# Part of one weight matrix moves from the SyncE queue's even spread to two GpSimd DMAs on seven DMA engines

## The chip, the cores and the metric

The kernel runs on one core of a Trainium2 chip. The metric is device time in microseconds (us) of one execution; lower is better. Before the change the median of three runs is 405.4 us (405.32 to 405.54).

## The reference

One decoding step (batch 1, one new token, model width 1024) of two blocks that share an input and whose outputs are added:

```
xn  = layernorm(x)                                   # 1024
A   = attention(xn @ wq, k_cache, v_cache) @ wo      # 32 query heads, 4 key/value heads, 65536 keys, 128 wide
B   : h  = gelu(layernorm(xn) @ w1)                  # 1024 x 1024
      hs = concat(four quarters of h, each shifted along the sequence and padded with zeros) @ w2   # 1024 x 1024
      x1 = xn + hs
      B  = x1 + gelu(layernorm(x1) @ w3) @ w4        # 1024 x 3584, 3584 x 1024
out = x + A + B
```

The sequence has length 1, so every shift by one or two positions leaves only the zero padding: the vector that is multiplied by w2 is zero, whatever h is. The kernel computes that product all the same. The data are bf16. Keys and values are 64 MiB each; the weights together are some 36 MB. All of it is read once.

## The kernel before

Everything is a stream of loads from HBM into eight buffers ("slots") of 128 partitions by 8192 bf16 values (16 KiB on each partition, 2 MiB in all), issued by SyncE in a fixed order: wq (two loads of two slots), w1, w2, w3 (two of two slots), then the four heads' keys and values in loads of two slots (4 MiB), where keys run five loads ahead of values, with wo's quarters among the last value loads, and w4 at the end. `issue` (it is called after each use of a slot) issues a load as soon as its slots are free, that is, when the TensorE or VectorE work that read the slot's last contents has signalled. So SyncE waits for slots, and up to eight slots of loads are queued on the DMA engines at any time. The last parts of w4 are issued in small pieces with a semaphore each (`load_pieces`, L306), so that its matmuls can begin piece by piece.

Uses go in the same order on the other engines. `rows_mv` (L424) multiplies a vector by rows of a weight matrix: partition p of a slot holds R = 8 consecutive rows, row kk of each is the moving operand, and four column ranges of 256 go to four row groups of PSUM. `to_p` (L428) brings the result back to partitions. Keys are transposed by VectorE into the tile `X` (two halves, L501) before TensorE takes them (L509); values are used from the slot (L549). `X` is [128, 2, 8192] bf16; half 1 also serves `to_p` (as `X32`, the same bytes seen as f32), and half 0 is first written when the first keys come.

`load_w2` does not exist yet: w2 is one load of one slot, `load(w2_v[:, 0:SLOT])` (L282), each partition taking 8 rows, 16 KiB in one run. `use_w2` multiplies it by `g_bf`, a tile of zeros that GpSimd clears at the start (the zero padding of the reference), and forms x1 and its layer norm.

GpSimd clears and fills constants at the start (L353 to L374) and computes one power in each of three layer norms (L410). ScalarE's queue issues the two loads of x: `xP_bf` (128 partitions of 16 bytes) and `xr_bf` (four partitions, 0, 32, 64 and 96, of 512 bytes), the second after VectorE has cleared `xr_bf` (L379). The first layer norm waits for both.

A wait before an instruction comes from `_deps`: it waits for the semaphores that stand in the buffers' records of writes and reads.

Of the kernel before, what the change touches and what calls it, by code (L numbers as in the profile page):

```python
# [6 lines left out]
BF = mybir.dt.bfloat16  # L7
F32 = mybir.dt.float32
# [66 lines left out]
def _deps(q, reads, writes):  # L75
    for b in reads:
        for s, v in b.w.items():
            q.wait((s, v))
    for b in writes:
        for s, v in b.w.items():  # L80
            q.wait((s, v))
        for s, v in b.r.items():
            q.wait((s, v))


def _done(ev, reads, writes, partial=False):
    for b in reads:
        b.add_read(ev)
    for b in writes:
        if partial:  # L90
            b.add_write(ev)
        else:
            b.set_write(ev)


def _op(q, fn, reads=(), writes=(), partial=False):
    _deps(q, reads, writes)
    ev = q.op(fn, True)
    _done(ev, reads, writes, partial)
    return ev  # L100


def _grp(q, fns, reads=(), writes=(), partial=False):
    _deps(q, reads, writes)
    ev = None
    for i, fn in enumerate(fns):
        ev = q.op(fn, i == len(fns) - 1)
    _done(ev, reads, writes, partial)
    return ev
# [8 lines left out]
def _dma(q, chan, fn, reads=(), writes=(), partial=False):  # L118
    _deps(q, reads, writes)
    chan.n += 1  # L120
    ev = q.dma(fn, chan.sem, 16 * chan.n)
    _done(ev, reads, writes, partial)
    return ev
# [10 lines left out]
def bass_parallel_sum__gqa_block_cached__mixer_s_mlp__decode_kernel(  # L134
# [14 lines left out]
    P = 128  # L149
    D = A_x.shape[2]  # L150
# [5 lines left out]
    R = D // P  # L156
# [6 lines left out]
    RW = D // 4  # L163
# [2 lines left out]
    SCALE = float(DH) ** -0.5  # L166
    EPS = 1e-5
    NS = 8
    SLOT = 8192

    with ExitStack() as es:
# [3 lines left out]
        def sb(name, shape, dt):  # L175
            return E(nc.sbuf_tensor(name, shape, dt))

        def ps(name, shape, dt):
            return E(nc.psum_tensor(name, shape, dt))

        def sem(name):
            return E(nc.semaphore(name))
# [24 lines left out]
        Yall = sb("Yall", [P, HKV, 4, 4, G], BF)  # L207
        slots_sb = sb("slots_sb", [P, NS, SLOT], BF)
        X = sb("X", [P, 2, SLOT], BF)
        S_sb = sb("S_sb", [P, NCH, 512], F32)  # L210
# [15 lines left out]
        g_bf = sb("g_bf", [P, R + 32], BF)  # L226
# [2 lines left out]
        ge_b = sb("ge_b", [P, NT], F32)  # L229
        h1g_bf = sb("h1g_bf", [P, R], BF)  # L230
        gh_bf = sb("gh_bf", [P, NT + 32], BF)
        fin = sb("fin", [P, RW], BF)

        S_all = ps("S_ps", [P, 4 * 512], F32)
# [4 lines left out]
        M1_ps = ps("M1_ps", [P, 512], F32)  # L239

        q_pe = _Q("pe", sem("c_pe"))
        q_dve = _Q("dve", sem("c_dve"))
        q_act = _Q("act", sem("c_act"))
        q_pool = _Q("pool", sem("c_pool"))
        q_sp = _Q("sp", None)
        ch_x = _DmaChan(sem("d_x"))
        ch_out = _DmaChan(sem("d_out"))
        slots = [_Slot(slots_sb[:, i, :], _B("slot%d" % i), _DmaChan(sem("d_s%d" % i))) for i in range(NS)]

        b_const = _B(); b_xb = _B(); b_x = _B(); b_xn = _B(); b_xn2 = _B(); b_x1 = _B(); b_xn3 = _B()  # L250
        b_ln = _B(); b_qT = _B(); b_Y = _B(); b_misc = _B(); b_ge = _B()
        b_X = [_B(), _B()]
# [5 lines left out]
        b_p = _B(); b_pT = _B(); b_lcol = [_B(), _B()]; b_OL = _B(); b_O = _B()  # L258
        b_cb = _B(); b_oP = [_B() for _ in range(HKV)]
        b_xr = _B(); b_accr = _B(); b_h1 = _B(); b_gh = _B(); b_fin = _B()  # L260


        place = [0]
        n_load = [0]
        taken = [0] * NS

        def room(n):
            p0 = place[0] + (place[0] % 2 if n == 2 else 0)
            return p0, all(taken[(p0 + i) % NS] == 0 for i in range(n))

        def take(n, uses):
            p0, free = room(n)
            assert free
            place[0] = p0 + n
            for i in range(n):
                taken[(p0 + i) % NS] = uses
            return p0 % NS

        def load(src, width=SLOT):
            i = take(1, 1)  # L280
            view = slots_sb[:, i, 0:width]
            _dma(q_sp, slots[i].chan, lambda e, view=view, src=src: e.dma_start(out=view, in_=src), writes=[slots[i].buf])  # L282
            return [(view, [slots[i].buf], i)]

        def load2(src, half=SLOT):
            i = take(2, 1)
            view = slots_sb[:, i:i + 2, :].rearrange("p s c -> p (s c)")[:, 0:2 * half]
            if 2 * half < 2 * SLOT:
                for k in range(2):
                    taken[i + k] = 2  # L290
            _dma(q_sp, slots[i].chan, lambda e, view=view, src=src: e.dma_start(out=view, in_=src), writes=[slots[i].buf, slots[i + 1].buf])  # L291
            bufs = [[slots[i].buf], [slots[i + 1].buf]] if half == SLOT else [[slots[i].buf, slots[i + 1].buf]] * 2
            return [(view[:, k * half:(k + 1) * half], bufs[k], i + k) for k in range(2)]
# [16 lines left out]

        wq_v = A_wq.rearrange("(p r) n -> p (r n)", p=P)
        w1_v = B_w1.rearrange("(p r) n -> p (r n)", p=P)
        w2_v = B_w2.rearrange("(p r) n -> p (r n)", p=P)
        w3_v = B_w3.rearrange("(p r) n -> p (r n)", p=P)
        w4_v = B_w4.rearrange("(p r) n -> p (r n)", p=P)

# [30 lines left out]
            return load2(A_v_cache[0, h, a * n:(a + 1) * n, :].rearrange("(p c) d -> p (c d)", p=P))  # L347


        evs = []  # L350
        for t_, val in ((selGT_bf, 1.0), (selTT, 1.0), (ident_bf, 0.0), (ones_f, 1.0), (neghalf, -0.5), (permWE, 1.0), (maskA, 1.0),
                        (sel16, 1.0), (dmask, 0.0), (g_bf, 0.0), (xn_bf, 0.0), (xn2_bf, 0.0), (xn3_bf, 0.0), (oP_bf, 0.0), (gh_bf, 0.0)):
# [22 lines left out]
                                                          compare_op=ALU.not_equal, fill=1.0, base=-16 * j, channel_multiplier=1))  # L375
        b_const.set_write(ev)

        _dma(q_act, ch_x, lambda e: e.dma_start(out=xP_bf[:, :], in_=A_x[0, 0, :].rearrange("(p r) -> p r", p=P)), writes=[b_xb])
        _op(q_dve, lambda e: e.memset(xr_bf[:], 0.0), writes=[b_xr])  # L379
        _dma(q_act, ch_x, lambda e: e.dma_start(out=xr_bf[0:P:32, :], in_=A_x[0, 0, :].rearrange("(j m) -> j m", j=4)), writes=[b_xr])  # L380
# [8 lines left out]
        def late_consts():  # L389
            _op(q_dve, lambda e: e.tensor_scalar(out=Lmat[:], in0=M1_ps[:, 0:P], scalar1=-SCALE, scalar2=None, op0=ALU.mult), reads=[b_M1], writes=[b_sel], partial=True)  # L390
            _op(q_dve, lambda e: e.tensor_copy(selT_f[:], M1_ps[:, 136:140]), reads=[b_M1], writes=[b_sel], partial=True)
            _op(q_dve, lambda e: e.tensor_copy(selL[:, :, :], M1_ps[:, P:P + 8].unsqueeze(2).broadcast_to([P, G, 16])), reads=[b_M1], writes=[b_sel], partial=True)
        xstep = X[:].ap[0][0]
        X32 = X[:].bitcast(F32)

        def layer_norm(src, b_src, dst_f, dst_bf, b_dst, c0):
            _op(q_dve, lambda e: e.reduce_sum(ln_s[:, 0:1], src[:], axis=AX.X), reads=[b_src], writes=[b_ln])
# [20 lines left out]
        def rows_mv(nkk, parts, st_fn, b_st, b_slot, b_out, first, last, k0=0):  # L418
            fns = []
            for kk in range(k0, k0 + nkk):  # L420
                for out_fn, mv_fn in parts:
                    for j in range(4):
                        fns.append(lambda e, kk=kk, j=j, out_fn=out_fn, mv_fn=mv_fn, st=(first and kk == k0), sp=(last and kk == k0 + nkk - 1):
                                   e.matmul(out_fn(j), st_fn(kk), mv_fn(kk, j), start=st, stop=sp, tile_position=(0, 32 * j), skip_group_check=True))  # L424
            _grp(q_pe, fns, reads=b_slot + [b_st], writes=b_out, partial=not first)

        def to_p(src, c0, n, b_src):
            _op(q_dve, lambda e: e.transpose(out=X32[:, 1, c0:c0 + 32 * n], in_=src), reads=b_src, writes=[b_X[1]], partial=c0 > 0)  # L428

# [9 lines left out]
        def use_wq(j, ld):  # L439
# [7 lines left out]
            for hf in range(2):  # L447
                to_p(S_ps[hf][:, :], 512 * hf, 16, [b_S[hf]])
            _op(q_dve, lambda e: e.tensor_copy(qT_bf[:], X32[:, 1, 0:1024:32]), reads=[b_X[1]], writes=[b_qT])
            _grp(q_pe, [lambda e, we=we: e.matmul(M0_ps[:, 128 + 32 * we:128 + 32 * we + HQ], permWE[:, we, :], qT_bf[:, :], start=True, stop=True)  # L450
# [8 lines left out]
        def d_parts(view, c0):  # L459
            return [(lambda t: M1_ps[32 * t:32 * t + 32, c0:c0 + RW], lambda kk, t: view[:, kk * D + t * RW:kk * D + (t + 1) * RW])]  # L460
# [6 lines left out]

        def use_w2(ld):
            view, b = ld[0:2]
            rows_mv(R, d_parts(view, 0), lambda kk: g_bf[:, kk:kk + 32], b_const, b, [b_M1], True, False)  # L470
            to_p(M1_ps[:, 0:RW].rearrange("p (c r) -> p r c", r=R), 0, R, [b_M1])
            _op(q_dve, lambda e: e.tensor_tensor(out=x1[:], in0=xn[:], in1=X32[:, 1, 0:32 * R:32], op=ALU.add), reads=[b_xn, b_X[1]], writes=[b_x1])
            layer_norm(x1, b_x1, None, xn3_bf, b_xn3, 4)
# [22 lines left out]
        def use_k(h, ch, ld):  # L496
# [3 lines left out]
            K32 = view.bitcast(F32)  # L500
            _op(q_dve, lambda e: e.transpose(out=X32[:, m, :], in_=K32), reads=b, writes=[b_X[m]])  # L501
            if ch % 2 == 0 and ch > 0:
# [73 lines left out]
        for kind, i in order:  # L576
# [3 lines left out]
            if kind == "v" and i in (8, 15):  # L580
                for n in ((0, 1) if i == 8 else (2, 3)):
# [6 lines left out]
        _op(q_dve, lambda e: e.tensor_scalar(out=accr[:], in0=xr_bf[:], scalar1=ln_s[:, 1:2], scalar2=ln_s[:, 4:5], op0=ALU.add, op1=ALU.mult),  # L588
            reads=[b_xr, b_ln], writes=[b_accr])
        _op(q_dve, lambda e: e.tensor_tensor(out=accr[:], in0=accr[:], in1=xr_bf[:], op=ALU.add), reads=[b_xr, b_accr], writes=[b_accr])  # L590
        loaders = {"wq": load_wq, "w1": lambda: load(w1_v[:, 0:SLOT]), "w2": lambda: load(w2_v[:, 0:SLOT]), "w3": load_w3, "wo": load_wo, "w4": load_w4,
                   "k": load_k, "v": load_v}
        doubles = {"wq", "w3", "k", "v"}

# [14 lines left out]
        for it in uses:  # L609
# [14 lines left out]
            elif kind == "v":  # L624
                h, n = args
# [48 lines left out]
```

## Time and profile before

| what | number |
|---|---|
| median of 3 runs | 405.4 us (405.32 to 405.54) |
| the profiled execution's own time | 405.31 us |
| its span, first to last instruction | 403.5 us |
| DMA: HBM read, mean rate | 169.87 MB, 421 GB/s |
| share of 16 DMA engines' span, SyncE's queue (q1) | 98.4% |
| VectorE busy | 183.8 us (46%) |
| TensorE busy, matmul and weight load | 152.1 us (38%) and 63.3 us (16%) |
| ScalarE busy | 75.9 us (19%) |
| GpSimd busy | 7.6 us (2%) |

The profile page shows one execution. Engines are PE (TensorE), PEld (its weight load), DVE (VectorE), ACT (ScalarE), POOL (GpSimd) and SP (SyncE). Sixteen DMA engines serve the core. A load of 128 partitions is cut into 128 packets, one for each partition, eight on each DMA engine, and every DMA engine adds one to the load's semaphore when its share has landed; the load is complete at sixteen. The trace holds, beside what the page sums up, the time of each of these increments ("landing records") and the queue, start, duration and size of each DMA packet ("packet records"); it doesn't say which DMA engine a packet ran on. Queue q1 is SyncE's, q10 ScalarE's; q8 and q14 carry instructions.

### The profile page before, as it was taken

The numbers are of one execution on the slowest core, as the hardware profiler recorded it, in microseconds if no ns is written. First come the engines' busy times: TensorE is split into PE (matmuls) and PEld (weight loads), VectorE is DVE, ScalarE is ACT, GpSimd is POOL, SyncE is SP. The second block draws the span as 40 slices with busy tenths as digits, with TensorE's granted clock in tenths as the row PEclk, the third lists the DMA queues.
The fourth block names the chain that finished last, engine by engine and source line by source line (L and its number), as shares of the span: only waits on it lengthen the run. The fifth ranks groups of instructions, "written<-read, shape, count | busy, mean of one in ns | idle before, by whom it ended". The sixth has DMA issues, their size and how long they took to land.

```text
span 403.5 us, 3693 instructions
## 1 busy us (share of the span) xinstructions
PE 152.1 (38%) x1615; PEld 63.3 (16%) x1615; DVE 183.8 (46%) x133; ACT 75.9 (19%) x71; POOL 7.6 (2%) x38
## 2 busy tenths in 40 slices
PE   0273333344247041345361514272141415262525
PEld 0132110001024010013110101141010101131213
DVE  0233019998837263755445465820817284100200
ACT  1000000111762010195010003830101014720000
POOL 5000000000000000000000000000000000000000
PEclk9995655555556656565856655657565655658656
DMA  9999999999999999999999999999999999999994
GB/s 364 416 416 434 447 416 427 452 416 426 445 427 416 440 442 416 426 453 419 424 438 435 416 437 439 422 422 437 435 421 432 438 426 434 429 435 408 439 406 190
DMA packets 7375, 170.10 MB, mean 422 GB/s; under 512 B 952, under 2 KB 960, under 8 KB 1856
## 3 DMA queue, kind: packets, MB, share of 16 engines
q1 hardware_dynamic: 7208, 169.87, 98.4%
q8 instruction: 12, 0.20, 0.2%
q10 hardware_dynamic: 152, 0.00, 0.0%
q14 instruction: 3, 0.02, 0.0%
HBM read 169.87 MB, written 0.00 MB: 421 GB/s over the span
## 4 chain that ended last, share of the span: by engine, by line
DMA 61%; DVE 15%; issue 8%; ACT 8%; PE 7%; SPq 1%; DVEq 0%; ACTq 0%
DMA slots_sb<-in_A_k_cache_dram 46%; DMA slots_sb<-in_B_w_dram 15%; DVE X L501 11%; ACT p_sb L529 5%; DVE mcol L517 4%; PE OT_ps L549 3%; PE PT_ps L535 2%; ACT pT_sb L538 2%; PE S_ps L509 1%; SPq L306 1%; PE M_ps L424 1%; ACT S_sb L518 0%; SPq L291 0%; SPq L282 0%; DVE fin L637 0%
## 5 line engine op out<-in xcount | busy, mean ns | idle before, releaser
L501 DVE STREAM_TRANSPOSE X<-slots_sb 128x4096 f32<-128x4096 f32 x32 | 141.2, 4428 | 98.6 <-DMA slots_sb<-in_A_k_cache_dram 98.6
L509 PE MATMUL S_ps<-X,Yall 128*32 128x512 bf16 x512 | 58.0, 602 | 148.0 <-DVE X L501 148.0
L518 ACT ACTIVATE S_sb<-S_ps 128x1024 f32<-128x1024 f32 x16 | 16.4, 1024 | 209.3 <-DVE mcol L517 209.3
L549 PE MATMUL OT_ps<-slots_sb,pT_sb 128*32 128x512 bf16 x512 | 45.5, 522 | 9.9 <-DMA slots_sb<-in_A_v_cache_dram 7.5
L509 PEld LDWEIGHTS S_ps<-X,Yall 128*32 128x32 bf16 x512 | 14.7, 125 | 186.7 <-DVE X L501 168.0
L529 ACT ACTIVATE p_sb<-S_sb,brun 128x1024 bf16<-128x1024 f32 x16 | 41.6, 2597 | 0.7
L535 PE MATMUL PT_ps<-ident_bf,p_sb 128*128 128x128 bf16 x128 | 16.6, 311 | 28.3 <-ACT oP_bf L566 14.7
L549 PEld LDWEIGHTS OT_ps<-slots_sb,pT_sb 128*32 128x32 bf16 x512 | 17.6, 126 | 34.2 <-issue 21.8
L517 DVE TENSOR_REDUCE mcol<-S_ps 128x1 f32<-128x1024 f32 x16 | 19.1, 1195 | 8.2 <-PE S_ps L509 8.2
L555 DVE TENSOR_TENSOR O_m<-OT_ps,selT_f 128x512 f32<-128x512 f32 x4 | 2.8, 690 | 41.3 <-PE OT_ps L549 41.3
L538 ACT ACTIVATE pT_sb<-PT_ps 128x1024 bf16<-128x1024 bf16 x16 | 16.4, 1024 | 18.1 <-PE PT_ps L535 18.1
L535 PEld LDWEIGHTS PT_ps<-ident_bf,p_sb 128*128 128x128 bf16 x128 | 12.4, 141 | 32.9 <-ACT pT_sb L538 16.6
L424 PE MATMUL S_ps<-slots_sb,xn_bf 128*32 128x512 bf16 (+1 forms) x128 | 12.8, 571 | 11.8 <-DMA slots_sb<-in_B_w_dram 10.3
L435 ACT ACTIVATE ge_a<-ge_b 128x8 f32<-128x8 f32 (+1 forms) x2 | 0.4, 217 | 52.1 <-DVE ge_b L434 52.1
L637 DVE TENSOR_TENSOR fin<-accr,M_ps 128x256 bf16<-128x256 f32 x1 | 0.4, 420 | 20.7 <-PE M_ps L424 20.7
L424 PE MATMUL M_ps<-slots_sb,gh_bf 128*32 128x256 bf16 x112 | 6.0, 376 | 9.9 <-DMA slots_sb<-in_B_w_dram 9.9
L428 DVE STREAM_TRANSPOSE X<-S_ps 128x512 f32<-128x512 f32 (+1 forms) x3 | 2.5, 850 | 15.6 <-PE S_ps L424 15.6
L424 PEld LDWEIGHTS S_ps<-slots_sb,xn_bf 128*32 128x32 bf16 x128 | 4.3, 133 | 18.2 <-DMA slots_sb<-in_B_w_dram 11.2
L424 PE MATMUL M_ps<-slots_sb,oP_bf 128*32 128x256 bf16 x128 | 5.4, 324 | 3.5 <-DMA slots_sb<-in_A_wo_dram 3.5
L382 DVE CAST xP<-xP_bf 128x8 f32<-128x8 bf16 x1 | 0.2, 171 | 14.1 <-DMA xr_bf<-in_A_x_dram 14.1
L424 PEld LDWEIGHTS M_ps<-slots_sb,gh_bf 128*32 128x32 bf16 x112 | 3.7, 131 | 12.5 <-DMA slots_sb<-in_B_w_dram 11.4
L559 PE MATMUL M_ps<-O_L,selL 128*128 128x129 f32 x8 | 2.0, 326 | 8.3 <-DVE O_L L558 8.3
(86 smaller groups left out, 54.4 us busy)
## 6 DMA issues: line engine op xcount, KB each, us to landing
slots_sb<-in_A_k_cache_dram SPq DMA_DIRECT2D x16, 4096.0 KB, 29.5
slots_sb<-in_A_v_cache_dram SPq DMA_DIRECT2D x16, 4096.0 KB, 31.2
slots_sb<-in_A_wq_dram SPq DMA_DIRECT2D x2, 4096.0 KB, 16.7
slots_sb<-in_A_wo_dram SPq DMA_DIRECT2D x4, 2048.0 KB, 25.2
slots_sb<-in_B_w_dram SPq DMA_DIRECT2D x2, 3584.0 KB, 33.7
slots_sb<-in_B_w_dram SPq DMA_DIRECT2D x2, 2048.0 KB, 28.0
slots_sb<-in_B_w_dram SPq DMA_DIRECT2D x1, 4096.0 KB, 28.6
slots_sb<-in_B_w_dram SPq DMA_DIRECT2D x5, 512.0 KB, 30.1
```

Of the source, the lines that this page charges most:

```text
L306: ev = q_sp.dma(lambda e, dst=dst, src=src: e.dma_start(out=dst, in_=src), ch.sem, 16 * ch.n)
L424: e.matmul(out_fn(j), st_fn(kk), mv_fn(kk, j), start=st, stop=sp, tile_position=(0, 32 * j), skip_group_check=True))
L428: _op(q_dve, lambda e: e.transpose(out=X32[:, 1, c0:c0 + 32 * n], in_=src), reads=b_src, writes=[b_X[1]], partial=c0 > 0)
L501: _op(q_dve, lambda e: e.transpose(out=X32[:, m, :], in_=K32), reads=b, writes=[b_X[m]])
L509: fns.append(lambda e, we=we, c_mid=c_mid, mv=mv: e.matmul(S_ps[bank][32 * c_mid:32 * c_mid + 32, :], Yall[:, h, we, :, :].rearrange("p a ...
L517: _op(q_dve, lambda e: e.reduce_max(mcol[:, x:x + 1], S2, axis=AX.X), reads=[b_S[2 * i], b_S[2 * i + 1]], writes=[b_mcol], partial=x > 0)
L518: _op(q_act, lambda e: e.activation(S_sb[:, 2 * x:2 * x + 2, :].rearrange("p s c -> p (s c)"), S2, ACTF.Copy), reads=[b_S[2 * i], b_S[2 * ...
L529: _op(q_act, lambda e, x=x: e.activation(p_sb[:, :, :, :, x], S_sb[:, 2 * x:2 * x + 2, :].rearrange("p s (c i) -> p s c i", i=32), ACTF.Ex ...
L535: _grp(q_pe, [lambda e, i=i, c=8 * c8 + i: e.transpose(out=PT_ps[:, i * P:(i + 1) * P], in_=p_sb[:, c // CL, c % CL, :, :].rearrange("p i ...
L538: _op(q_act, lambda e, c8=c8: e.activation(pT_sb[:, :, 32 * c8:32 * c8 + 32, :].rearrange("p a x g -> p x a g"), PT_ps[:, :].rearrange("p ...
L549: fns.append(lambda e, cl=cl, q4=q4, x0=x0: e.matmul(OT_ps[32 * q4:32 * q4 + 32, :], pT_sb[:, a, x0:x0 + 4, :].rearrange("p x g -> p (x g) ...
L555: _op(q_dve, lambda e: e.tensor_tensor(out=O_m[:, :, :], in0=OT_ps[:, :].rearrange("p (t d) -> p t d", t=4), in1=selT_f[:, :].unsqueeze(2) ...
```

## The change

Of the 1024 rows of w2, SyncE's main load takes 768 (six on each of 128 partitions, 12 KiB in one run). Rows 992 to 1023 come by a second SyncE DMA into the same slot, behind the six rows: 128 partitions of a quarter row, 512 bytes each. The 224 rows between go to the half 0 of `X`, 8 rows (16 KiB in one run) on each of 28 partitions, by two DMAs that GpSimd issues: 160 rows to partitions 0 to 19, with a source whose outermost size is 5, and 64 rows to partitions 60 to 67, with an outermost size of 2. After the first stands a DMA of a few bytes of x with an outermost size of 2, after the second one with an outermost size of 7; their destination `pad_sb` is not read. VectorE clears half 0 of `X` at the start, ahead of its clearing of `xr_bf`, and GpSimd waits for that. `use_w2` multiplies the zeros of `g_bf` by the six rows of the slot, then by all eight rows of `X` half 0 on all partitions, then by the quarter rows, all into the same sums.

```diff
@@ names and tiles
+    W2B = 6
+    W2Q = 992
+        pad_sb = sb("pad_sb", [8, 4, 8], BF)
+        ch_w2 = _DmaChan(sem("d_w2"))
+        ch_q = _DmaChan(sem("d_q"))
@@ views
-        w2_v = B_w2.rearrange("(p r) n -> p (r n)", p=P)
+        w2_v = B_w2[0:W2B * P, :].rearrange("(p r) n -> p (r n)", p=P)
+        w2_q = B_w2[W2Q:D, :].rearrange("f (t n) -> (f t) n", t=4)
@@ loads
+        def load_w2():
+            got = load(w2_v, W2B * D)
+            sl = slots[got[0][2]]
+            ch_q.n += 1
+            sl.buf.add_write(q_sp.dma(lambda e: e.dma_start(out=sl.view[:, W2B * D:W2B * D + RW], in_=w2_q), ch_q.sem, 16 * ch_q.n))
+            return [(sl.view, [sl.buf], got[0][2])]
+
+        def load_w2_part(p0, k, row):
+            n = 4 * k * R
+            src = B_w2[row:row + n, :].rearrange("(b a r) n -> a b (r n)", a=k, b=4)
+            dst = X[p0:p0 + 4 * k, 0, :]
+            ch_w2.n += 1
+            q_pool.dma(lambda e: e.dma_start(out=dst, in_=src), ch_w2.sem, 16 * ch_w2.n)
+            return row + n
+
+        def load_pad(k, at):
+            src = A_x[0, 0, 0:16 * k].rearrange("(a b c) -> a b c", a=k, b=2)[:, :, 0:4]
+            dst = pad_sb[0:k, at:at + 2, 0:4]
+            ch_w2.n += 1
+            q_pool.dma(lambda e: e.dma_start(out=dst, in_=src), ch_w2.sem, 16 * ch_w2.n)
+
+        def load_w2_parts():
+            _deps(q_pool, [], [b_X[0]])
+            row = load_w2_part(0, 5, W2B * P)
+            load_pad(2, 0)
+            row = load_w2_part(60, 2, row)
+            load_pad(7, 2)
+            assert row == W2Q
+            b_X[0].add_write((ch_w2.sem, 16 * ch_w2.n))
@@ start, after GpSimd's constants
+        _op(q_dve, lambda e: e.memset(X32[:, 0, :], 0.0), writes=[b_X[0]])
+        load_w2_parts()
@@ use_w2
-            rows_mv(R, d_parts(view, 0), lambda kk: g_bf[:, kk:kk + 32], b_const, b, [b_M1], True, False)
+            rows_mv(W2B, d_parts(view, 0), lambda kk: g_bf[:, kk:kk + 32], b_const, b, [b_M1], True, False)
+            rows_mv(R, d_parts(X[:, 0, :], 0), lambda kk: g_bf[:, kk:kk + 32], b_const, [b_X[0]], [b_M1], False, False)
+            rows_mv(1, [(lambda t: M1_ps[32 * t:32 * t + 32, 0:RW], lambda kk, t: view[:, W2B * D:W2B * D + RW])], lambda kk: g_bf[:, 0:32], b_const, b, [b_M1], False, False)
@@ loaders
-        loaders = {... "w2": lambda: load(w2_v[:, 0:SLOT]), ...}
+        loaders = {... "w2": load_w2, ...}
```

More of the change, by code (lines that the diff above doesn't have):

```diff
@@ L260, in bass_parallel_sum__gqa_block_cached__mixer_s_mlp__decode_kernel @@
         b_xr = _B(); b_accr = _B(); b_h1 = _B(); b_gh = _B(); b_fin = _B()
+        xstep = X[:].ap[0][0]
+        X32 = X[:].bitcast(F32)
         place = [0]
@@ L392, in late_consts @@
             _op(q_dve, lambda e: e.tensor_copy(selL[:, :, :], M1_ps[:, P:P + 8].unsqueeze(2).broadcast_to([P, G, 16])), reads=[b_M1], writes=[b_sel], partial=True)
-        xstep = X[:].ap[0][0]
-        X32 = X[:].bitcast(F32)
         def layer_norm(src, b_src, dst_f, dst_bf, b_dst, c0):
@@ L590, in bass_parallel_sum__gqa_block_cached__mixer_s_mlp__decode_kernel @@
         _op(q_dve, lambda e: e.tensor_tensor(out=accr[:], in0=accr[:], in1=xr_bf[:], op=ALU.add), reads=[b_xr, b_accr], writes=[b_accr])
-        loaders = {"wq": load_wq, "w1": lambda: load(w1_v[:, 0:SLOT]), "w2": lambda: load(w2_v[:, 0:SLOT]), "w3": load_w3, "wo": load_wo, "w4": load_w4,
+        loaders = {"wq": load_wq, "w1": lambda: load(w1_v[:, 0:SLOT]), "w2": load_w2, "w3": load_w3, "wo": load_wo, "w4": load_w4,
                    "k": load_k, "v": load_v}
```

## The prediction

> **What bounds the kernel now.** I read the page's time slices and queue table first, then the chain, then the DMA view of the last microseconds, then SyncE's waits.
>
> ```profile
> span 403.5 us, 3693 instructions
> ...
> DMA  9999999999999999999999999999999999999994
> ...
> q1 hardware_dynamic: 7208, 169.87, 98.4%
> q8 instruction: 12, 0.20, 0.2%
> ...
> q14 instruction: 3, 0.02, 0.0%
> ```
>
> The DMA row is 9 in every slice but the last; SyncE's queue alone fills 98.4% of sixteen engines' span. No compute engine passes 46%. Hence only bytes per DMA engine can move the end, unless a queue runs dry. The two instruction queues matter below.
>
> The chain in order of time ends so:
>
> ```profile
> 368.50 32.03 DMA slots_sb<-in_B_w_dram
> 400.53 0.04 issue
> 400.57 0.44 PE M_ps L424 x4
> 401.01 0.02 issue
> 401.03 0.42 DVE fin L637
> ```
>
> The last piece of w4 was issued early and lands at 400.53; what follows is fixed work of 3 us. The DMA view from 396 to 401 us, 40 slices of 0.125 us by packets' starts, shows how the sixteen engines get there:
>
> ```profile
> DMA  9999999875686655555532222232222100000000
> ...
> q1 hardware_dynamic: 382, 0.88, 45.7%
> ```
>
> The share falls in steps: about half of the engines work from 397.3 to 398.4, a quarter until 400. The landing records of that last piece say the same: 397.25, 397.40, 397.41, 397.42, 397.63, 397.96, 398.17, 398.43 (eight engines), then 398.99 to 399.16 (four), then 400.43 to 400.53 (four). So **four engines set the end**, and the earliest is 3.3 us ahead of them. The packet records say why: packets of an engine follow each other without a gap, so each one's sequence can be followed by its phase. The 12 instruction packets of q8 (16 KiB) hit eight engines, the four last ones twice, the next four once; each takes 1.02 to 1.11 us and the packet behind it about 0.5 us more (1.61 instead of 1.07 at 34.87), 1.57 in all. The three of q14 (8 KiB) cost 0.7 us each, on three of the other engines. Engines that are near in phase can be mistaken for each other in this, but the groups of 8, 4 and 4 also stand in the landing records.
>
> That loads are queued deep enough is read from SyncE's waits and the chain:
>
> ```profile
> SPq L48 <- DVE X L501: 195.2, 16, 18.0
> ```
>
> ```profile
> 34.47 35.78 DMA slots_sb<-in_A_k_cache_dram
> ...
> 128.88 28.89 DMA slots_sb<-in_A_k_cache_dram
> ```
>
> SyncE spends its time waiting for slots, and a load that it issues lands 29 to 36 us later, though 4 MiB take 9.7 us at the measured rate: some 19 us of other loads are always ahead of it.
>
> **The change part by part.** *The slot's load, on every engine.* Starts of consecutive packets lie 0.611 us apart at 16 KiB and 0.159 at 4 KiB; on the line between them 12 KiB take 0.460. Eight packets: 4.89 before, 3.68 after. The quarter rows add eight packets of 512 bytes; the four such packets of xr_bf delayed their engines by 0.024 each, so 0.19, and a semaphore write 0.006. Each engine saves 1.21 - 0.20 = **1.0 us**. SyncE's extra issue (0.33 to 0.65 us for a load in the trace) delays the w3 loads, which would otherwise be queued 25 us early.
>
> *The 224 rows.* 28 packets of 16 KiB on seven engines are four on each. Bound from below: 4 x 0.611 = 2.44 us, as SyncE's. From above: as q8's packets of the same size, 4 x 1.57 = 6.28. I take 2.44, since these go from HBM to the same partitions as SyncE's; 16-byte packets of the second hardware queue were interleaved with SyncE's at 10 us without loss. A seven's net change is 2.44 - 1.0 = **+1.44 us**, at most +5.3. The few-byte DMAs: two packets of 0.01 on each engine they use.
>
> *Which seven.* The sizes 5, 2, 2, 7 would place them on five engines in a row, skip two, take two, and skip seven, sixteen in all. The trace has no GpSimd DMA, so it doesn't show which engine comes first. Two things bear on it. The four xr_bf packets fall at phases (13.485, 13.502, 13.509, 13.543) of which at least three belong to engines that q8 never hits; and eight engines stay free of q8, so that seven can be chosen among them. [...] I take it that the seven are among the eight free engines.
>
> *The end.* The four late engines land at 400.53 - 1.0 = 399.53. The sevens land at 397.25 + 1.44 = 398.7 up to 398.43 + 1.44 = 399.87, if the latest free one (its phase is that of an xr_bf packet, and its q14 packet came at 80.43) is among them and is hit again; else 398.17 + 1.44 = 399.61. So the gain is 0.66 in the first case and 0.92 to 1.0 in the others. I take **0.8**, between them, since the q14 packets are three events on three engines and need not fall alike. 405.31 - 0.8 = 404.5 for the profiled execution; it lies 0.09 below the median of 405.4, so the forecast is **404.6 us**.
>
> *VectorE's clearing of X half 0*, 4096 values of f32 on each partition: between 0.17 us (its memset of 128) and 4.43 (a transpose of this size); I take 4.4. It stands ahead of the clearing of xr_bf, so ScalarE's second issue moves from 1.24 to about 5.5. Nothing else is behind it there, and it costs nothing: xr_bf's packets were served only after xP_bf's eight on each engine, at 13.5, one per turn of 1.21 us. Without that cover it would cost the 4.3 us in the head only.
>
> *GpSimd's issues.* They stand behind the constants (done at 8.01) and ahead of the first power at 17.97, in an idle time of 9.96 us, which holds four issues of up to 2.4 us (SyncE's are 0.33 to 1.07). On xr_bf's engines four 16 KiB packets may come in turn with x's, which lands up to 2.4 us later, at 17.6, and with it the layer norm, q and the use of w1. [...]
>
> *PE.* use_w2's matmuls grow from 32 to 60; 32 took 1.93 us, so 28 more take 1.7, between 32.46 and 38. x1's layer norm, which waits for them, was done at 38.5 and is waited for by w3's matmuls, which waited for DMA until 42.33. The slots of w1 and w2 come free 1.7 later plus the head's 2.4, so the second keys load is issued at 38.6 instead of 34.47; the engines have loads queued until the first keys land at 60.5. So the head has about 20 us of cover; a delay beyond it would cost its excess one for one. The 28 weight loads and 28 matmuls add 56 PE instructions; the q8 packets lie some 256 apart, and the last came with about 226 to go, so a thirteenth could come near the end, on an engine hit once: 399.16 + 1.57 - 1.0 = 399.7, still no later than the above.
>
> [...]
>
> **The rivals.** (1) *The extra 64 KiB fall on a late engine*: the order of engines is not as I take it. For: nothing in the trace names the first engine, and four of sixteen are late. Against: the order 5, skip 2, 2 avoids something. Price: 400.53 + 1.44 = 401.97, slower by 1.44: 406.8. It decides as soon as one of the four is among the seven. (2) *GpSimd's packets are dear*, as q8's are: between 1.07 and 1.57 us each, +3.3 to +5.3 on the seven; 398.43 + 3.3 = 401.7, to 403.7: 406.6 to 408.6. It passes the late engines' old end from 0.78 us a packet (398.43 + 4 x 0.78 - 1.0 = 400.55). For: the same size on another queue took that long. Against: SyncE's 768 packets of this size took 0.611 to 0.621 each, to the same kind of place. (3) *An engine hit once takes the extra*, 399.16 + 1.44 = 400.6, or instruction packets fall otherwise: no change, 405.3 to 405.5. (4) *The four late ones are not always the same*, and the gain is that of the last of the sevens alone, 0.4 to 0.6: 404.9.
>
> **How the numbers follow.** I call 0.2% (0.8 us, a limit of 404.59) what a measurement tells from no change. Forecast 0.62, its own range 404.3 to 404.9, split 0.40 below the limit and 0.22 above; (1) 0.15; (2) 0.15; (3) and (4) 0.08. Faster 0.40, same 0.30, slower 0.30. The range takes in (1) and the lower part of (2): 404.2 to 406.9.
>
> **What would show it.** The last piece's landings should lie within 1 us rather than 3.3, the last near 399.7; the DMA view of the last 5 us should stay near 9 until 398.5 and then drop at once. Step by step: w2's packets at 0.46 us; 28 packets of 16 KiB on a new queue at 0.61; x landing by 17.6; the last q8 engines 1.0 earlier. I am wrong if some engines end later than 400.5 with the new packets on them, if these take over 0.78 us, or if DMA is idle anywhere before 397.

## The result and the profile after

The changed kernel takes 404.79 us (median of 22 runs, 404.56 to 405.10) against 405.40 us before (22 runs, 405.29 to 405.73): a ratio of 0.9985, 95% interval 0.9979 to 0.9991. That is 0.61 us, 0.15%: a gain that the interval tells from nothing, but below the 0.2% that the prediction called the limit. Of the prediction's own range of 404.3 to 404.9 it lies in the part above that limit, which had the smaller share of the chance. The profiled execution took 404.61 us, its span 402.8.

The page of the changed kernel, its time slices and queue table:

```profile
span 402.8 us, 3756 instructions
...
DMA  8999999999999999999999999999999999999995
...
q1 hardware_dynamic: 7352, 169.42, 98.3%
q0 software_dynamic: 224, 0.46, 0.3%
q8 instruction: 13, 0.21, 0.2%
...
q14 instruction: 3, 0.02, 0.0%
```

The 0.46 MB have moved from SyncE's queue q1 to GpSimd's, q0. DMA is still at 9 everywhere but at the ends, and there is a thirteenth instruction packet on q8. The chain of the changed kernel in order of time (start, length, what) ends so:

```profile
373.33 26.61 DMA slots_sb<-in_B_w_dram
399.94 0.04 issue
399.98 0.32 PE M_ps L464 x4
400.30 0.02 issue
400.33 0.42 DVE fin L679
```

It is the same chain as before, and its load lands at 399.94 instead of 400.53: 0.59 of the 0.70 us by which the two profiled executions differ. The DMA view of the changed kernel from 396 to 401 us, in slices of 0.125 us:

```profile
DMA  9999999889989796667544443210000000000000
...
q1 hardware_dynamic: 414, 0.98, 50.7%
q8 instruction: 1, 0.02, 1.4%
```

Before, the row stood at about 2 from 398.6 to 399.9 and ended at 400; now it stays at 7 to 9 until 397.9 and falls to 0 at 399.4, and SyncE's queue moves 0.98 MB in the stretch instead of 0.88. The landing records of the last piece, one for each engine, are 396.82, then fifteen from 398.12 to 399.94 (398.12, .16, .30, .34, .80, .94, .97, 399.00, .50, .55, .65, .78, .85, .88, 399.94). Eight engines were done by 398.43 before; now it is five. The engines are evened out, not level.

The head, in the changed kernel's timeline (start, duration, engine, line, operation; the bracket is the idle time before it):

```profile
1.72 3.47 DVE L418 MEMSET X<- 128x4096 f32 x1 [1.72 <-PEq L701]
...
5.36 1.07 ACTq L422 DMA_DIRECT2D xr_bf<-in_A_x_dram  x1
...
8.49 0.78 POOL L371 DMA_DIRECT2D X<-in_B_w_dram  x1 [0.46 <-issue]
9.26 0.57 POOL L378 DMA_DIRECT2D pad_sb<-in_A_x_dram  x1
9.82 0.58 POOL L371 DMA_DIRECT2D X<-in_B_w_dram  x1
10.39 0.56 POOL L378 DMA_DIRECT2D pad_sb<-in_A_x_dram  x1
15.77 0.17 DVE L424 CAST xP<-xP_bf 128x8 f32<-128x8 bf16 x1 [10.45 <-DMA xr_bf<-in_A_x_dram]
```

x is there at 15.75 instead of 15.16, in spite of a clearing of 3.47 us ahead of it. The 28 packets of 16 KiB on q0 each take 0.611 us, most of the 12 KiB packets of the slot's load 0.460 or 0.464.

### The profile page after: what moved, and what is told of

Read it like the earlier page. It is cut to its first block, busy times and chain, and to the rows that moved or that the text cites. A ratio compares the mean times of both kernels' runs of the same rounds, so it can differ in the third digit from the quotient of the medians.

```text
span 402.8 us, 3756 instructions
## 1 busy us (share of the span) xinstructions
PE 156.2 (39%) x1643; PEld 64.9 (16%) x1643; DVE 187.5 (47%) x134; ACT 76.0 (19%) x71; POOL 10.1 (3%) x42
## 4 chain that ended last, share of the span: by engine, by line
DMA 65%; issue 11%; DVE 11%; PE 6%; ACT 4%; SPq 2%; POOLq 0%; POOL 0%; DVEq 0%; ACTq 0%
DMA slots_sb<-in_A_k_cache_dram 52%; DVE X L543 8%; DMA slots_sb<-in_B_w_dram 7%; DMA slots_sb<-in_A_wq_dram 6%; DVE mcol L559 3%; PE OT_ps L591 3%; ACT p_sb L571 3%; SPq L314 2%; PE S_ps L464 1%; PE PT_ps L577 1%; ACT pT_sb L580 1%; PE S_ps L551 1%; ACT S_sb L560 0%; PE M_ps L446 0%; POOLq L173 0%
## 5 line engine op out<-in xcount | busy, mean ns | idle before, releaser
L560 ACT ACTIVATE S_sb<-S_ps 128x1024 f32<-128x1024 f32 x16 | 16.4, 1023 | 208.6 <-DVE mcol L559 208.6
L591 PE MATMUL OT_ps<-slots_sb,pT_sb 128*32 128x512 bf16 x512 | 47.0, 536 | 9.5 <-DMA slots_sb<-in_A_v_cache_dram 7.1
L580 ACT ACTIVATE pT_sb<-PT_ps 128x1024 bf16<-128x1024 bf16 x16 | 16.4, 1024 | 18.1 <-PE PT_ps L577 18.1
L464 PE MATMUL S_ps<-slots_sb,xn_bf 128*32 128x512 bf16 (+1 forms) x128 | 13.7, 602 | 9.5 <-DMA slots_sb<-in_B_w_dram 5.2
```

Source lines behind the costliest of these rows:

```text
L560: _op(q_act, lambda e: e.activation(S_sb[:, 2 * x:2 * x + 2, :].rearrange("p s c -> p (s c)"), S2, ACTF.Copy), reads=[b_S[2 * i], b_S[2 * ...
L580: _op(q_act, lambda e, c8=c8: e.activation(pT_sb[:, :, 32 * c8:32 * c8 + 32, :].rearrange("p a x g -> p x a g"), PT_ps[:, :].rearrange("p ...
L591: fns.append(lambda e, cl=cl, q4=q4, x0=x0: e.matmul(OT_ps[32 * q4:32 * q4 + 32, :], pT_sb[:, a, x0:x0 + 4, :].rearrange("p x g -> p (x g) ...
```

## The experiments

The engines below are counted from 0 in the order in which GpSimd's DMAs take them; the packet records don't name engines, so engines are told apart by following the packets of each by their phase. In the code, `...` marks lines that are left out.

**Taking away the instruction packets (e4, the kernel before).** The theory says that the four late engines are late because q8's packets hit them twice.

```diff
-            for cl in range(CL):
+            if n > 0:
+                return
+            for cl in range(4):
...
-                dict(w1=use_w1, w2=use_w2, w3=use_w3, wo=use_wo, w4=use_w4)[kind](*args, ld)
+                if kind != "wo":
+                    dict(w1=use_w1, w2=use_w2, w3=use_w3, wo=lambda *a: None, w4=use_w4)[kind](*args, ld)
```

> The kernel before with 624 of TensorE's 1615 matmuls left out (nearly all of the products of probabilities and values, and all of the products with wo), so that the output is not the reference's; every load stays. Theory (the four late engines are late by a second 16 KiB packet of TensorE's instructions, 1.57 us each): with some 1250 TensorE instructions fewer, 8 instruction packets come instead of 12, one on each of eight engines, none twice; the last landing is 399.0 to 399.2 instead of 400.5 and the time 404.0 (403.8 to 404.2). Rival (four engines are slower in themselves, or by their place): 405.4, the last landings in the same groups.

403.97 us (403.87 to 404.00), ratio 0.9965 (0.9952 to 0.9978). Its page, and its DMA view from 396 to 401 us:

```profile
q8 instruction: 8, 0.13, 0.1%
```

```profile
DMA  9999899975566555444320400000000000000000
```

With eight instruction packets instead of twelve, none a second one on its engine, the long tail at 2 is gone and the last landing is 399.20 instead of 400.53. All loads are as before. e4 also leaves TensorE less work, but the landing records of the full kernel show the packets' effect by themselves. From the load whose last landing is 383.09 to the one that lands at 392.84, fifteen engines of the kernel before move on by 9.74 us and one by 11.30, and the packet of 387.13 lies between. Nine of its twelve q8 packets stand alone between two loads in this way, and each moves one landing by 1.54 to 1.57 us more than the rest; the other three fall together with other changes. Before the twelfth packet the landings stand in groups of eight, five and three engines, after it in groups of eight, four and four. So it is the second packet on four engines that set the end, and the mechanism of the prediction's first part is shown.

**The other seven engines (e1, then e5).** In e1 the tiny DMAs are put ahead, so that the same two loads, to the same partitions, fall on engines 5, 6 and 9 to 13.

```diff
...
-            row = load_w2_part(0, 5, W2B * P)
-            load_pad(2, 0)
-            row = load_w2_part(60, 2, row)
-            load_pad(7, 2)
+            load_pad(5, 0)
+            row = load_w2_part(60, 2, W2B * P)
+            load_pad(2, 2)
+            row = load_w2_part(0, 5, row)
+            load_pad(2, 4)
```

> The change with its four GpSimd DMAs in another order: few-byte one of size 5, the 64-row one of size 2, few-byte one of size 2, the 160-row one of size 5, few-byte one of size 2. Bytes, instructions and destinations are the changed kernel's; only which seven DMA engines carry the 64 KiB differs. Theory (the end is that of the DMA engines which the instruction packets of q8 made late, so what counts is which engines get the bytes): of the nine engines that the change spares, seven now carry 2.44 us more, among them at least two that were hit twice; these landed last at 399.5 to 399.9 in the changed kernel, so the last landing comes at 401.9 to 402.4 and the time is 406.8 to 407.3, slower than before by 1.4 to 1.9 us. Rival (the gain comes from a second queue, or from fewer bytes on SyncE's, whichever engines carry them): 404.8, as the changed kernel.

411.68 us (411.46 to 412.53), ratio 1.0159 (1.0144 to 1.0174): slower by 6.3 us, far beyond both prices that were named. The 16 KiB packets on q0 took 0.866 us (median; 0.611 to 1.213), and SyncE's own packets of that time were longer too (32 KiB packets that start from 16 to 22 us: 1.22 to 1.88 us, in the changed kernel 1.21). So something else than the load on late engines was at work. The other difference to the changed kernel is which engines write which partitions of SBUF: partitions 0 to 19 and 60 to 67 are written by engines 0 to 4, 7 and 8 there, and by 9 to 13, 5 and 6 here. That each engine writes partitions of its own for SyncE is the author's reading; the packet records name neither engine nor partition, so it can be tried only by the price. e5 uses e1's engines, with partitions 20 to 27 and 68 to 87 (the code is against e1).

```diff
-            row = load_w2_part(60, 2, W2B * P)
+            row = load_w2_part(20, 2, W2B * P)
             load_pad(2, 2)
-            row = load_w2_part(0, 5, row)
+            row = load_w2_part(68, 5, row)
```

> The other seven engines of the first experiment again, but with destinations moved: the 64 rows to partitions 20 to 27, the 160 rows to partitions 68 to 87. [...] Theory (two effects in the first experiment: late engines loaded, and packets slowed where two engines write the same group of partitions): the packets take 0.611 us again, the last landing comes at 401.9 to 402.4, the time is 406.8 to 407.3. Rival (the 4.5 us beyond that came from loading late engines, wherever they write): 411.7.

407.11 us (406.98 to 407.19), ratio 1.0041 (1.0026 to 1.0056). The 16 KiB packets on q0 are back at 0.611 to 0.621. The end of its chain and its DMA view from 396 to 403 us (slices of 0.175 us):

```profile
375.52 26.61 DMA slots_sb<-in_B_w_dram
402.14 0.04 issue
```

```profile
DMA  8777555554554554555454461121111100000000
```

The last landing is 402.14, and the tail at 1 at the end of the view is three engines (401.89, 402.06, 402.14), with the others at 400.70 or earlier. Both are as the theory said. This is what loading late engines costs: 1.7 us against the kernel before.

**The same seven engines, with e5's partitions (e7, the changed kernel).**

```diff
-            row = load_w2_part(0, 5, W2B * P)
+            row = load_w2_part(68, 5, W2B * P)
             load_pad(2, 0)
-            row = load_w2_part(60, 2, row)
+            row = load_w2_part(20, 2, row)
```

> The changed kernel with only the destinations changed: its 160 rows to partitions 68 to 87 and its 64 rows to 20 to 27, on the same seven engines as in the changed kernel. Theory (an engine that writes partitions which another engine is writing slows both): packets of 16 KiB over 0.611 us on GpSimd's queue and longer ones on SyncE's while they last, some 3 to 5 us lost before 45 us, time 407.5 to 409.5. Rival (where the rows go doesn't matter, only which engines carry them): 404.8.

409.88 us (409.47 to 410.17), ratio 1.0107 (1.0090 to 1.0124): 5.1 us slower than the changed kernel with the same engines, packets and bytes, and 0.4 above what the theory expected at most. The DMA views from 10 to 35 us, first of the changed kernel, then of e7:

```profile
DMA packets 952, 10.58 MB, mean 423 GB/s; under 512 B 335, under 2 KB 467, under 8 KB 467
...
q0 software_dynamic: 224, 0.46, 4.7%
```

```profile
DMA packets 688, 8.41 MB, mean 336 GB/s; under 512 B 302, under 2 KB 306, under 8 KB 306
...
q0 software_dynamic: 224, 0.46, 6.7%
```

and the same of e5 and of e1:

```profile
DMA packets 977, 10.48 MB, mean 419 GB/s; under 512 B 363, under 2 KB 495, under 8 KB 495
...
q0 software_dynamic: 256, 0.46, 4.8%
```

```profile
DMA packets 719, 8.39 MB, mean 336 GB/s; under 512 B 333, under 2 KB 337, under 8 KB 337
...
q0 software_dynamic: 256, 0.46, 6.7%
```

In these 25 us, in which the new packets run, the sixteen engines together move 336 GB/s in e7 and e1 instead of 423 and 419. The 2.17 MB that e7 lacks against the changed kernel are 5.1 us at 423 GB/s; its last landing is 405.24 against 399.94, 5.3 later. For e1 against e5 it is 2.09 MB, 5.0 us, and 406.82 against 402.14, 4.7. It isn't the new packets alone: from 16 to 22 us all 55 of SyncE's 32 KiB packets in e7 took 1.38 to 1.92 us; in the changed kernel all 70 took 1.21. Engines, sizes and bytes are the same in the two kernels, so the place alone makes this difference; so it does from e5 to e1.

**An even spread (e2, then e6).** One GpSimd DMA gives 7 rows to each of 32 partitions, 14 KiB, two packets on every engine. If balance is all, this must give nothing.

```diff
...
+            src = B_w2[row:row + 224, :].rearrange("(p r) n -> p (r n)", p=32)
+            dst = X[0:32, 0, 0:7 * D]
...
-            row = load_w2_part(0, 5, W2B * P)
-            load_pad(2, 0)
-            row = load_w2_part(60, 2, row)
-            load_pad(7, 2)
+            row = load_w2_even(W2B * P)
```

> The change, but the 224 rows come by one GpSimd DMA over 32 partitions of 7 rows each (14 KiB in one run), two packets on each of sixteen engines, without the few-byte DMAs. Theory: every engine saves 1.0 us and gets 2 x 0.53 us back, so the four late ones end where they ended before (last landing 400.5 to 400.6), time 405.3 to 405.6, with the last landings spread over 3 us again. Rival (a GpSimd queue or a shorter w2 load helps in itself): 404.8.

408.88 us (408.52 to 409.20), ratio 1.0083 (1.0066 to 1.0100): neither price. Its 14 KiB packets took 0.535 to 1.436 us, median 1.18. Sixteen engines wrote partitions 0 to 31; in the changed kernel engines 0 to 4 wrote 0 to 19 at 0.611 us for 16 KiB, and in e5 engines 5 and 6 wrote 20 to 27 at 0.611 to 0.621. e6 makes it two DMAs on eight engines each, to partitions 0 to 31 and 64 to 95, half rows:

```diff
...
+            src = B_w2[row:row + 112, :].rearrange("f (h n) -> (f h) n", h=2).rearrange("(b a r) n -> a b (r n)", a=8, b=4)
+            dst = X[p0:p0 + 32, 0, 0:7 * D // 2]
...
+            row = load_w2_half(0, W2B * P)
+            row = load_w2_half(64, row)
```

> The even spread again, by two GpSimd DMAs of outermost size 8, each to 32 partitions of 7 half rows (7 KiB in one run): partitions 0 to 31 on the first eight engines and 64 to 95 on the last eight, four packets on each engine, in the partitions that it also writes for SyncE. Theory: packets at their own price (0.27 us), each engine gets 1.1 us back for the 1.0 it saves, the four late engines end as before, 405.3 to 405.6. Rival (a GpSimd DMA on all sixteen engines costs 3.5 us in itself): 408.9.

405.91 us (405.75 to 406.11), ratio 1.0012 (1.0003 to 1.0021). Every 7 KiB packet on q0 takes 0.272 us, and 3 us of e2's loss are gone. The last landing is 400.71, 0.2 later than before, and four engines are again later than the rest (400.55 to 400.71). So e2's loss fits the place, though e6 also has other packet sizes and two DMAs for one, and it is e5 and e7 that show the place by itself. Moving these bytes to another queue evenly gained nothing: e6 is 0.5 us slower than the kernel before, 0.3 beyond what was expected at most. Some 0.3 us of that lie outside the span (its own time is 2.13 us over its span, 1.8 in the kernels before and after); that part is open.

**Which engine is first (e3, the kernel before).** Sixteen small GpSimd DMAs of two packets each, every one with packets of its own size.

```diff
...
+        for i in range(16):
+            w = 256 + 16 * i
+            src = A_k_cache[0, 0, 0:24, :].rearrange("(a b) d -> a (b d)", a=3).rearrange("a (b n) -> a b n", b=2)[:, :, 0:w]
+            dst = X[2 * i:2 * i + 2, 0, 0:3 * w]
+            ch_m.n += 1
+            q_pool.dma(lambda e, dst=dst, src=src: e.dma_start(out=dst, in_=src), ch_m.sem, 16 * ch_m.n)
...
```

> The kernel before with sixteen small GpSimd DMAs at the start, each on one DMA engine and each with packets of a size of its own (six of 512 to 992 bytes), to read which DMA engine carries which sequence of packets. If GpSimd's DMAs go round the engines from 0, marker i is on engine i; then the xr_bf packets should stand with markers 0 to 3, and the eight engines that q8 hits should be eight of 5, 6 and 9 to 15. If the cursor starts elsewhere or does not go round, the xr_bf packets stand with other markers. Time as before, 405.3 to 405.8, by either.

406.34 us in a single execution, 0.5 above what was expected; one execution doesn't tell why. Each marker came as one packet on each of two engines (1536 to 2976 bytes), not as six on one. Markers 0 and 1 stand 0.02 us behind the four packets of `xr_bf`, on the same phases, and where the phases can be followed safely, markers i and i + 8 fall on the same pair of engines: in this run GpSimd's DMAs start where `xr_bf`'s lie and go round the sixteen, two engines for each marker.

**Without the 224 rows (e10), and the changed kernel again (e11).** e10 leaves out the GpSimd DMAs and so the seven engines' extra load; e11 is the changed kernel itself, beside it on the same chip.

```diff
-        load_w2_parts()
```

> The changed kernel without its GpSimd DMAs: the 224 rows are not loaded at all (448 KiB less), the matmuls on X half 0 and all else stay. Theory (in the changed kernel the four late engines and the latest of the seven end together, at 399.9): the seven fall back to 397.3 to 398.0 at the last landing, the four late ones stay at 399.5 to 399.9, and the time is 404.6 to 404.8, hardly below the changed kernel's. Rival (the seven alone set its end): 404.3 or less.

> The changed kernel itself, beside the two others on the same chip: 404.7 to 404.9.

404.49 us (404.33 to 404.56), ratio 0.9976 (0.9966 to 0.9985), and 404.89 us (404.63 to 404.99), ratio 0.9985 (0.9977 to 0.9994). The DMA view of e10 from 396 to 401 us:

```profile
DMA  9566675555548332222223210000000000000000
```

About four engines work from 398 on, as before the change, and their last landing is 399.76; the seven are done at 396.4 to 397.6. Against the changed kernel's 399.94 this says that both groups end together there: taking the sevens' whole extra load away brings only another 0.4 us. The time lies between the theory's 404.6 to 404.8 and the rival's 404.3 or less, nearer to the theory.

**A longer head (e8, the kernel before).** Six clearings of `X` half 0 instead of the change's one, ahead of `xr_bf`'s, to find out how much the head can be delayed.

```diff
...
+        for _ in range(6):
+            _op(q_dve, lambda e: e.memset(X32[:, 0, :], 0.0), writes=[b_X[0]])
...
```

> The kernel before with VectorE's clearing of X half 0 alone, six times over (6 x 3.47 = 20.8 us), ahead of the clearing of xr_bf; nothing else of the change. x lands at 23 to 25 instead of 15.2, so the first layer norm, q, and the slots of wq, w1 and w2 come 8 to 10 us later. Theory (loads are queued some 20 us deep in the head, so a delay there is covered): 405.4, no change. Rival (the head's delay reaches the end): 412 to 415.

407.39 us (407.22 to 409.06; the last is the profiled execution), ratio 1.0057 (1.0037 to 1.0077). Two of its six clearings in the timeline, and the windows of 10 us (busy time of PE, PEld, DVE, ACT and POOL, TensorE's granted clock, DMA share, GB/s), of the kernel before and then of e8:

```profile
1.71 3.47 DVE L382 MEMSET X<- 128x4096 f32 x1 [1.71 <-PEq L660]
6.10 3.47 DVE L382 MEMSET X<- 128x4096 f32 x1 [0.92 <-DVE X L382]
```

```profile
40.00:50.00 10.00, 3.16 (x32) 1.10 (x32) 0.00 (x0) 0.00 (x0) 0.00 (x0) 0.67 1.00 432
```

```profile
40.00:50.00 10.00, 6.47 (x112) 3.69 (x108) 4.85 (x18) 0.21 (x1) 0.55 (x1) 0.92 0.73 281
```

Neither price came. Each clearing that waited for the one ahead cost 0.92 us more, 4.6 in all; `xr_bf` was issued at 27.31, and the last of its packets landed at 34.33. So x came 19.2 us later than its 15.16, and not 8 to 10 as was meant. The engines then ran dry from 40 to 50 us (share 0.73). What came late is w3's second load, issued at 41.91 instead of about 23: it waits for the slots of the weights ahead of it. A delay of 19.2 cost 2.0 us, 3.7 in the profiled execution. If what goes beyond the cover costs its own length, an estimate from these figures is a cover of 15.5 to 17 us.

**A third group (e9).** The slot's load is cut to five rows, SyncE's quarter rows become half rows, and 96 rows go to partitions 80 to 95 on engines 12 to 15 (the same pairs as in e6, where a packet of 7 KiB took 0.272 us): a try at evening out the rest.

```diff
-    W2B = 6
-    W2Q = 992
+    W2B = 5
+    W2Q = 960
...
-            load_pad(7, 2)
+            load_pad(3, 2)
+            row = load_w2_part(80, 4, row, 6)
```

> A finer balance on the changed kernel. SyncE's w2 load takes five rows on each partition (640) and half a row of 64 more (1 KiB on each partition, in place of the quarter rows); the 224 rows go to the same seven engines; 96 rows go to partitions 80 to 95 by a further GpSimd DMA of outermost size 4, six rows on each, so to the last four engines, which by the earlier runs are hit by q8 once or never and ended at 397.8 or earlier. The second few-byte DMA has size 3, so that all sizes sum to 16. Every engine saves a further 0.6 and pays 0.2 more for its small packets: late four and seven about 0.4 earlier (399.05 where they ended at 399.45), the last four engines at 397.8 - 0.4 + 4 x 0.46 = 399.2. Theory (bytes per engine set the end): 0.25 us below the changed kernel's time of the same call, some 404.5. Rival (the rest of the spread is chance, from where instruction packets fall): 404.8, no difference.

406.12 us (404.60 to 406.47), ratio 1.0007 (0.9997 to 1.0017). The twelve times fall into two groups, four at 404.60 to 404.98 and eight at 405.94 to 406.47; the profiled execution is the longest. Its DMA view from 396 to 401 us:

```profile
DMA  9999979999899868665444312111160000000000
```

Most engines end by 399.6, but one lands at 401.11 alone, 0.95 behind the next. The landing records say why in this execution. The engine carries the third group's extra rows (at 33 us it lands some 1.8 us behind the five engines without any) and was then hit twice by q8: by the first packet, at 35.57 (its landing moved by 1.57 us more than the others', from 32.79 to 42.89), and, if the packets go round eight engines here too, by the ninth, at 279.51. Between the loads that end at 275.69 and 286.36 one landing went from 275.07 or 275.09 to 286.36, 1.55 to 1.58 us more than the rest, and from there to 401.11. The expectation took these four engines to be hit once or never. The two groups of times lie 1.5 us apart, about one such packet; that in the four shorter ones the second packet fell on another engine is not shown, since only the longest was profiled. Neither expected time came for the kernel as a whole: the four shorter times (404.7) are 0.2 below the changed kernel's 404.89, the eight others about 1.3 above it, and so it is no better than the changed one.

## Why the prediction was right, point by point

*What bounds the kernel.* Right, and shown by e4: without the second packet on four engines the time is 1.4 us shorter with the loads untouched. The prices were nearly right: the landing records give 1.54 to 1.57 us for a q8 packet (1.57 taken), and 0.94, 0.68 and 0.72 for the three q14 packets of the changed kernel (0.7 taken).

*The slot's load, 1.0 us on every engine.* The prices held: starts mostly 0.460 us apart at 12 KiB, 0.023 to 0.024 at 512 bytes. In e10, where nothing but this load was cut, the four late engines landed 1.00, 0.93, 0.93 and 0.77 earlier, in order, so the term is right to 0.1 for three of them. In the changed kernel they came down by less, by 0.6 to 0.9: landings at 399.5 to 399.9 instead of 400.43 to 400.53. No packet price accounts for the missing 0.1 to 0.4; what does isn't shown.

*The 224 rows, 4 x 0.611.* Right: all 28 packets took 0.611. The reason given, that they go "from HBM to the same partitions as SyncE's", was too loose. It is true of e7 and e1 as well, and there the packets took 0.85 and 0.87 us (medians) and the core's whole stream lost 5 us. In these runs the price holds with the changed kernel's and e5's pairs of engines and partitions (0.611 to 0.621 us) and is lost when they are exchanged; that the good pairs are those of SyncE's own loads, as e6's expectation has it, is the author's reading: it fits all of these prices, and no record shows it directly. The case that the second rival priced from 0.78 us a packet up lies next to the changed kernel, with two partition numbers changed; its price of 406.6 to 408.6 was even too low, since it counted the new packets alone and not SyncE's beside them.

*Which seven.* Right, though nothing in the trace before shows where GpSimd's DMAs begin, so that the seven were the author's choice. In the changed kernel four of the first five 16 KiB packets of q0 (13.489, 13.507, 13.538 and 13.576) start 0.023 to 0.024 us behind the four of `xr_bf` (13.465, 13.483, 13.515 and 13.552), the three q14 packets are on loaded engines, and q8 stays on its eight. e3 shows that GpSimd's DMAs began at `xr_bf`'s engines; e5 shows the first rival's price, 401.97 and 406.8 us, as 402.14 and 407.11.

*The end.* The choice between the cases was the miss in size. The first case, the latest of the seven being the engine with an `xr_bf` and a q14 packet, was worked out as 399.87, a gain of 0.66. It is what came: 399.94, and 0.61 us; followed back through the landing records, the last engine is one of the seven that had a q14 packet. I took 0.8, halfway to the other cases, and so 404.6 instead of 404.79. The other side of it, the late four, came to 399.9 as well instead of 399.53, so the two groups tie; the time alone would not tell this from the fourth rival's 404.9, the landings do. Nor does it say much that the time fell in the range as a whole, 404.2 to 406.9, which held no change and a slowdown too; what carries the prediction are the packets and the landings.

*The landings' spread.* The sign named beforehand, all landings within 1 us, failed: they span 3.1 us, fifteen of them 1.8. Nor did the DMA view stay near 9 until 398.5 and drop at once: it fell from 397.9 to 399.4. The free engine without extra rows and the once-hit ones stay early; that costs nothing.

*VectorE's clearing.* 3.47 us instead of 4.4, hidden as said (a second one behind it, in e8, starts 4.39 us after the first). x came 0.6 later instead of up to 2.4: GpSimd's issues took 0.56 to 0.78 us, and the first 16 KiB packets of q0 started only at 13.42. The cover that was named, about 20 us, is 15.5 to 17 by the estimate from e8, and the load that runs dry first is w3's second and not the second keys load. For a head that moved by 0.6 us this made no difference.

*The thirteenth instruction packet.* The twelve of the kernel before start 172 to 330 TensorE instructions apart, 248 on average ("some 256" in the prediction). A thirteenth came, at 397.77, but it cost almost nothing: its engine had all but finished. From the last piece but one to the last, one landing moved 0.13 us more than the others' 0.65, and the once-hit engines landed at 398.12 to 398.34. So the 399.7 that was worked out, with a full 1.57 in it, was 1.4 too late. By luck of timing, not by its price, this packet stayed out of the end.

*A second queue in itself.* It gives nothing here: in e6 the same bytes, spread evenly over the engines, gain nothing (0.5 us slower), and no engine was slower than another with GpSimd's DMAs, since all 64 packets, four on each engine, took 0.272 us. The changed kernel gains because it spreads the bytes unevenly, to the engines that had time left.

## What to carry to other kernels

When the DMA queue is full to the end, read the sixteen landing records of the last load: the spread between them is what uneven work on the engines costs, and here it came from instruction packets that nobody placed. Moving bytes to the engines with time left can bring the end down to the mean of that spread at most, and stops helping when the next group ties. When a DMA is steered to engines of one's own choice, the partitions that it writes must be tried too, by its packets' times and by those of the main stream beside them: the wrong partitions cost 5.1 us here (e7), eight times the 0.61 that the balance brought.

## What the runs showed of the hardware that was not expected

**Which engine writes which partitions changed the price of the whole stream.** With the same engines and bytes, 448 KiB to other partitions cost 5.1 us (e7 against the changed kernel), 4.6 (e1 against e5) and 3.0 (e2 against e6). The first two pairs show that the destination does it, since nothing else differs in them; the third differs in packet sizes too. How it does so is not shown. Packets of 16 KiB took up to 1.21 us in e1 and 1.25 in e7, about twice 0.611, and SyncE's 32 KiB packets from 16 to 22 us took 1.22 to 1.88 and 1.38 to 1.92 us instead of 1.21.

**Instruction packets went round eight engines.** By the landing records q8's packets went round eight of the sixteen in the changed kernel (the ninth and tenth on the engines of the first and second), and nine of the twelve in the kernel before cost their engines 1.54 to 1.57 us each, in a stream without gaps. Their number went with TensorE's instructions: 8 packets with 991 matmuls (e4), 12 with 1615, 13 with 1643. No run here shows what they cost the engine that issues; on the DMA engines that carry them they set the end of the kernel before (400.53 with twelve, 399.20 with eight).

**A clearing that waited for the one ahead** started 0.92 us after that one's end, seen five times in e8, so that six of 3.47 us took 25.4.
